# Raw q and k of each head in a tile of its own, two buffers, loaded one head ahead

## The chip, the cores and the metric

The kernel runs on one core of a Trainium2 chip. The metric is the device time of one execution in microseconds (us); the median of three runs is given with its extremes. The core has five engines that run their own instruction streams and wait for each other by semaphores: TensorE (PE; its weight loads are listed as PEld), VectorE (DVE), ScalarE (ACT), GpSimd (POOL) and SyncE (SP). In this kernel SP does nothing but issue DMA transfers, in the order of its stream. A transposition (DMA_TRANSPOSE) is such a transfer too.

## What is computed

Attention with a decay, causal, over 4 batches of 8 heads, 576 positions, head width 64; its output is the input of four experts that are all computed and mixed with given weights.

```python
scores = (q @ k.T) / 8 + (cum[:, None] - cum[None, :])   # cum = cumsum(log(clip(f, 1e-4, 1)))
scores = where(causal, -1e9, scores)
attn   = exp(scores - max(scores)); attn /= sum(attn) + 1e-9
x      = (attn @ v)  -> [2304, 512]                      # 4 x 576 rows, 8 heads x 64
p      = domain_probs / (sum + 1e-9)
out    = sum over e of p[:, e] * (relu(x @ w1[e]) @ w2[e])   # 4 experts, 512 -> 1024 -> 512
```

## The kernel before, in words

**Jobs.** Attention is cut into 32 jobs (`JOBS`, line 42): first, batch by batch, the rows 0 to 255 (half 0), then, batch by batch, the rows 256 to 575 (half 1); within each, four pairs of heads (`pr` 0 to 3, heads `hh` 0 and 1). A name as `pt_2_1_1` is pair 2, half 1, head 1; the digit of the batch is left out where names are printed. In this text, **pair 1 to pair 16** are the jobs of half 1 in the order in which they run: pairs 1 to 4 are batch 0, pairs 5 to 8 batch 1, and so on.

**One head.** Its q and k lie in `raw` (float32, in transposed form, with k below q's positions along the row). ScalarE rounds them to `hi` (line 558), GpSimd makes a copy of q (559) and the remainder of k, `kl` (567; two rows of `kl` with the running decay come by DMA from `ncd`, line 533). PE makes the scores s from `hi` and from `kl` (611), VectorE masks them and takes the row maximum (`p`, `nm`, 625), ScalarE takes exp (640), and ScalarE and VectorE split the result into two float16 halves `z` (706, 707). Three transpositions per head, for the row tiles 2, 3 and 4, turn `z` into `pt` (716, on SP's queue; `z` is 128x6x128, 128x8x128 and 128x9x64). When both heads of a pair are there, PE multiplies `pt` with `v`: 28 matmuls o (809), of which one runs early and 26 or 27 stand together as the **main group o** of the pair, behind the pair's last transposition, which is the 9x64 one of head 1. The result is scaled into `xf` (856).

**The experts.** Four pairs fill a chunk of x. VectorE takes its maximum (`xmax`, 260), a scale is made over PE and back (`topx`, 199 and 220; `ux`, 202 to 232; `xsc`, 249), and ScalarE and VectorE write the chunk as two float16 halves `y` (474, 475). From `y` and the weights PE makes the first layer of the experts (matmuls l, lines 1002 and 1035), with ScalarE and VectorE behind it (`gh`, `gl`, 1015, 1016; `acc`, 1062). Weights come by DMA and are prepared meanwhile (`wr`, `pk`, `wd`, `w`; `wmax` 284; a scale of the weights by `dw` and `tops`, 316 and 317: `dw` goes out to memory, `tops` reads it back). The second half of the execution is the experts alone.

**Loads of `raw`.** The first four jobs' q and k lie in buffers that are free at the start (`first_raw`). From the fifth on `Job.load` (line 505) loads both heads of a job at once into a tile of 128x2x896 float32 of which there is one buffer: 12 loads of 512 KB (half 0), 16 of 896 KB (half 1), each followed by the load of the job's v (`vr`). Since there is one buffer, the transfer of the next job waits until both heads of the job before have been read by ScalarE (558) and GpSimd (559, 567).

**What sets the order.** `head_steps(n)` (line 876) lists the steps that are written while head n is at work: preparation of head n+1, the decay rows of head n+2 (`far`), the load of head n+2's job if that is its first head, then scores, transpositions and o. The steps of the experts are put between them. The order on every engine is then made by the framework's scheduler, which simulates the program's times and takes, on each engine, what it expects to be ready (`schedule_with_timeline_sim=True`, line 1752): other durations or buffers in one place can change the order everywhere, and each engine runs strictly in the order it was given.

Of the kernel before, what the change touches and what calls it, by code (L numbers as in the profile page):

```python
# [8 lines left out]
F32 = mybir.dt.float32  # L9
# [69 lines left out]
def fused(ctx: ExitStack, tc: tile.TileContext, qk, v, f, probs, w, out):  # L79
# [57 lines left out]
    def decays():  # L137
        nc.sync.dma_start(out=fr, in_=f)
        first_loads()
        for t in q2:  # L140
            nc.gpsimd.memset(t[64:66, :].bitcast(F32), 8.0)
        make_identity(nc, ident)
        nc.gpsimd.memset(ones_r, 1.0)
        nc.vector.memset(ones, 1.0)
        nc.vector.tensor_scalar(
            out=fr, in0=fr, scalar1=1e-4, scalar2=1.0, op0=ALU.max, op1=ALU.min
        )
        nc.scalar.activation(out=fr, in_=fr, func=AF.Ln)
        nc.scalar.activation(out=warm, in_=ones[:, :1], func=AF.Exp)
        nc.vector.tensor_tensor_scan(  # L150
            out=ncum, data0=ones, data1=fr, initial=0.0, op0=ALU.mult, op1=ALU.subtract
        )
        nc.scalar.activation(out=nc2[0], in_=ncum, func=AF.Copy)
        nc.vector.tensor_tensor(
            out=nc2[1], in0=ncum, in1=nc2[0].bitcast(F32), op=ALU.subtract
        )
        nc.gpsimd.memset(mask, 0.0)
        nc.gpsimd.affine_select(
            out=mask[:, S - 128 :],
            in_=mask[:, S - 128 :],  # L160
            pattern=[[-1, 128]],
            compare_op=ALU.is_ge,
            fill=NEG,
            base=0,
            channel_multiplier=1,
        )
        for h in range(NEAR):
            jobs[0].near(h)
        for n in range(2):
            nc.sync.dma_start(out=ncd[:, n], in_=nc2[n].bitcast(F32))  # L170
        first_raw(2)
        for j in (0, 2):
            n = 1 if j == 0 else 0
            nc.sync.dma_start(
                out=first_kl[j // 2][64:66, 512 * n :].bitcast(F32).rearrange(
                    "p (h s) -> p h s", s=CH
                ),
                in_=ncd[2 * (j + n) : 2 * (j + 2), :, :CH].rearrange("h n s -> n h s"),
            )
        first_raw(3)  # L180
        w_load(0)
        w_load(1)
        nc.sync.dma_start(out=pr_r, in_=probs)
        jobs[NPR].load()
        for hh in range(2):
            jobs[NPR].far(hh)

    later = {}
# [239 lines left out]
    def first_loads():  # L428

        slots = [  # L430
            x_.tile([128, 1024], F32, tag=t, name=f"first{n}")
            for n, (x_, t) in enumerate([(xf_p, f"xf{k}") for k in range(3)] + [(acc_p, "acc")] * 2)
        ]
        for n in range(2):
            first_kl.append(acc_p.tile([128, 1024], F32R, tag="acc", name=f"kl{n}"))
        vt = slots[3].rearrange("p (r t h d) -> p r t h d", r=NPR, t=2, h=2)
        for j in jobs[:NPR]:
            r = slots[(4, 0, 1, 2)[j.pr]]
            j.raw = r.rearrange("p (h n) -> p h n", h=2)
            j.vr = vt[:, j.pr]  # L440
        first_raw(0)
        nc.sync.dma_start(
            out=slots[3].rearrange("p (r n) -> p r n", r=NPR),
            in_=v[0, :, :, :2].rearrange("r p t h d -> p r (t h d)"),
        )
        first_raw(1)

    def first_raw(n):
        j = jobs[n]
        nc.sync.dma_start(out=j.raw, in_=qk[0, j.pr, :, :, : 2 * CH])  # L450

    xh, xl, xf = {}, {}, {}
    yh, yl = {}, {}
# [38 lines left out]
    class Job:  # L492


        def __init__(self, b, pr, half):
# [4 lines left out]
            self.njt = 2 if half == 0 else 5  # L500
            self.nm = f"{b}_{pr}_{half}"
            self.hi, self.kl, self.q2, self.p, self.nmax = {}, {}, {}, {}, {}
            self.sp, self.last, self.pt, self.tp, self.op = {}, {}, {}, {}, {}

        def load(self):
            b, pr = self.b, self.pr
            n = self.wq + self.wk
            o = 0 if self.half == 0 else CH
            self.raw = raw_p.tile([128, 2, 896], F32, tag="raw", name=f"raw{self.nm}")
            nc.sync.dma_start(out=self.raw[:, :, :n], in_=qk[b, pr, :, :, o : o + n])  # L510
            self.vr = v_p.tile([128, 5, 2, D], F32, tag="vr", name=f"vr{self.nm}", bufs=1)
            nc.sync.dma_start(out=self.vr[:, : self.njt], in_=v[b, pr, :, : self.njt])

        def rows(self, hh):

# [36 lines left out]

        def prep_hi(self, hh):
            wq, wk = self.wq, self.wk
            r = self.raw[:, hh, :]
            hi = hi_p.tile([128, 896], F32R, tag="hi", name=f"hi{self.nm}_{hh}")
            self.hi[hh] = hi
            nc.scalar.activation(out=hi[:, : wq + wk], in_=r[:, : wq + wk], func=AF.Copy)  # L558
# [2 lines left out]
        def prep_lo(self, hh):  # L561
            if hh not in self.kl:
                self.rows(hh)
            wq, wk, ko, qo = self.wq, self.wk, self.ko, self.qo
            r, hi, kl = self.raw[:, hh, :], self.hi[hh], self.kl[hh]
            eng = nc.vector if self is jobs[0] else nc.gpsimd
            eng.tensor_tensor(  # L567
                out=kl[:64, :wk],
# [307 lines left out]
    def head_steps(n):  # L876
# [9 lines left out]
        if n + 2 < len(heads):  # L886
            j, hh = heads[n + 2]
            st.append((0, lambda j=j, hh=hh: j.far(hh)))
        ahead = n + 2 < len(heads) and heads[n + 2][1] == 0
        if ahead:  # L890
            st.append((0, heads[n + 2][0].load))
        qs, ts, us = [], [], []
        if n < len(heads):
            j, hh = heads[n]
# [861 lines left out]
```

## Time and profile before

| | us |
| --- | --- |
| median of 3 runs | 963.48 (958.53 to 964.21) |
| profiled execution | 963.1 |
| its span in the trace | 961.3 |

| engine | busy us | share of the span | instructions |
| --- | --- | --- | --- |
| PE | 895.0 | 93% | 5831 |
| VectorE | 713.9 | 74% | 1458 |
| ScalarE | 559.3 | 58% | 1121 |
| GpSimd | 537.6 | 56% | 544 |

The profiled execution took 1.8 us more than its span, the time from the first recorded instruction to the last. The mean granted clock of PE over the span is 0.988 of full speed. A busy share is an average over stages: attention and the experts' first layer run together up to about 630 us, and the experts alone after that. "Releaser" in a row is what an engine's wait ended with; a row of a timeline with "x27" is so many instructions in succession. In a row of SP's queue the duration is the issue, not the transfer.

### The profile page before, as it was taken

How to read it: one execution, taken by the hardware profiler on the slowest of the kernel's cores; microseconds unless marked ns; L12 is line 12 of the kernel's file. 1: busy time of each engine (PE TensorE's matmuls, PEld its weight loads, DVE VectorE, ACT ScalarE, POOL GpSimd, SP SyncE). 2: the span in 40 equal slices, each digit the busy share in tenths (PEclk: the TensorE clock that was granted, in tenths of full speed). 3: DMA queues.
4: the chain of work that ended last, by engine and by line, in shares of the span. 5: the costliest groups of instructions: out<-in, count | busy, mean ns of one | idle time of the engine just before them, and what ended most of it. 6: DMA issues, size and time to landing. Idle time of an engine off the chain costs nothing.

```text
span 961.3 us, 16609 instructions
## 1 busy us (share of the span) xinstructions
PE 895.0 (93%) x5831; PEld 631.1 (66%) x5831; DVE 713.9 (74%) x1458; ACT 559.3 (58%) x1121; POOL 537.6 (56%) x544
## 2 busy tenths in 40 slices
PE   4799998999998889889899999999998999999998
PEld 3699897999765557556566666654455664566547
DVE  5777675876987988668887877575678847787487
ACT  5777755465767657557566676255656436653350
POOL 4656864567634646325654576163877826686060
PEclk9999999999999999989999999999999999999999
DMA  7458734538989689965998599424313422322003
GB/s 246 140 191 296 254 113 163 187 117 277 279 210 188 175 253 241 226 157 136 259 306 205 116 266 284 117 83 154 110 44 117 147 88 87 111 80 98 23 1 88
DMA packets 147060, 159.45 MB, mean 166 GB/s; under 512 B 85700, under 2 KB 106880, under 8 KB 146976
## 3 DMA queue, kind: packets, MB, share of 16 engines
q1 hardware_dynamic: 146976, 158.39, 57.0%
q8 instruction: 46, 0.75, 0.3%
q14 instruction: 38, 0.31, 0.1%
HBM read 117.30 MB, written 21.65 MB: 145 GB/s over the span
## 4 chain that ended last, share of the span: by engine, by line
PE 19%; POOL 12%; DVE 7%; ACT 5%; issue 4%; DMA 4%; POOLq 0%; DVEq 0%; SPq 0%
PE y L1273 6%; PE m L1273 6%; POOL s L1333 4%; POOL wt L1167 4%; PE l L1002 3%; PE l L1035 3%; POOL wu L1167 2%; DMA pk<-in_w 1%; POOL bs L1199 1%; DVE rl L1154 1%; DMA wr<-in_w 1%; ACT wt L1194 1%; ACT r L1319 1%; DVE acc L1062 1%; DMA raw<-in_qk 1%
## 5 line engine op out<-in xcount | busy, mean ns | idle before, releaser
L1002 PE MATMUL l<-y,w 128*128 128x256 f16 x1248 | 155.9, 275 | 0.0
L640 ACT ACTIVATE p<-p,nm 128x576 f32<-128x576 f32 (+3 forms) x160 | 95.7, 599 | 92.1 <-DVE nm L625 91.3
L1002 PEld LDWEIGHTS <-w 128*128 128x128 f16 x1248 | 118.1, 98 | 30.8 <-issue 6.4
L1035 PE MATMUL l<-w,gh 128*128 128x512 f16 x408 | 123.9, 383 | 5.5 <-ACT w L969 2.8
L707 DVE SCALAR_TENSOR_TENSOR z<-p,z 128x384 f16<-128x384 f32 (+3 forms) x128 | 86.5, 694 | 25.9 <-ACT z L706 24.2
L559 POOL CAST q<-raw 64x320 fp32r<-64x320 f32 (+1 forms) x56 | 27.8, 497 | 127.6 <-PE s L611 63.0
L611 PE MATMUL s<-hi 128*128 128x384 f32 (+1 forms) x192 | 76.7, 403 | 17.0 <-DVE hi L573 8.9
L1062 DVE SCALAR_TENSOR_TENSOR acc<-y,scg,acc 128x256 f32<-128x256 f32 (+1 forms) x164 | 81.1, 515 | 14.9 <-PE y L1273 14.7
L1273 PE MATMUL m<-rh,bs 128*128 128x512 f16 x256 | 86.5, 379 | 3.0 <-ACT r L1319 3.0
L1199 POOL TENSOR_TENSOR bs<-wt,bs 128x512 f16<-128x512 f32 x32 | 38.1, 1194 | 80.4 <-ACT bs L1198 80.2
L625 DVE CUSTOM_DVE_ANT_0 p<-s,mask 128x288 f32<-128x288 f32 (+2 forms) x160 | 74.3, 473 | 10.0 <-PE s L611 9.4
L567 POOL TENSOR_TENSOR kl<-raw,hi 64x576 fp32r<-64x576 f32 (+1 forms) x56 | 66.6, 1189 | 25.5 <-ACT hi L558 24.8
L1035 PE MATMUL l<-w,gl 128*128 128x512 f16 x204 | 77.5, 382 | 0.0
L946 POOL TENSOR_TENSOR wl<-wr,wh 128x512 fp32r<-128x512 f32 x48 | 64.4, 1367 | 16.2 <-ACT wh L942 9.9
L1016 DVE SCALAR_TENSOR_TENSOR gl<-l,gh 128x512 f16<-128x512 f32 (+1 forms) x80 | 54.7, 683 | 25.0 <-ACT gh L1015 24.9
L961 POOL TENSOR_SCALAR wr<-wr,wsc 128x512 f32<-128x512 f32 x32 | 52.5, 1645 | 34.0 <-DMA wr<-in_w 27.8
L1002 PE MATMUL l<-xl,wh 128*128 128x256 f32 x224 | 66.7, 298 | 0.1
L1002 PE MATMUL l<-xh,wh 128*128 128x256 f32 x224 | 66.0, 297 | 0.4
L1273 PE MATMUL m<-rh,bw 128*128 128x512 f16 x191 | 65.2, 383 | 0.8 <-ACT r L1319 0.8
L1002 PE MATMUL l<-xh,wl 128*128 128x256 f32 x224 | 65.7, 293 | 0.0
L1273 PEld LDWEIGHTS <-bs 128*128 128x128 f16 x384 | 37.6, 98 | 41.6 <-issue 3.2
L1035 PEld LDWEIGHTS <-gh 128*128 128x128 f16 x408 | 37.4, 99 | 41.5 <-issue 12.3
(387 smaller groups left out, 2415.6 us busy)
## 6 DMA issues: line engine op xcount, KB each, us to landing
wr<-in_w SPq DMA_DIRECT2D x90, 512.0 KB
pk<-in_w SPq DMA_DIRECT2D x64, 256.0 KB
wd<-w SPq DMA_DIRECT2D x32, 512.0 KB
raw<-in_qk SPq DMA_DIRECT2D x16, 896.0 KB
bw<-wd SPq DMA_DIRECT2D x32, 256.0 KB
bv<-wd SPq DMA_DIRECT2D x32, 256.0 KB
raw<-in_qk SPq DMA_DIRECT2D x12, 512.0 KB
vp<-in_v SPq DMA_DIRECT2D x10, 512.0 KB
```

What stands on the lines that cost most here:

```text
L567: eng.tensor_tensor(out=kl[:64, :wk], in0=r[:64, ko : ko + wk], in1=hi[:64, ko : ko + wk].bitcast(F32), op=ALU.subtract,)
L611: nc.tensor.matmul(out=ps[:, at : at + z - a], lhsT=lhsT, rhs=rhs, start=(m == 0), stop=(m == 1),)
L625: nc.vector.tensor_tensor_reduce(out=pt[:, a:z], in0=ps, in1=mask[:, m0 + a : m0 + z], scale=-0.125, scalar=BIG if n == 0 else nm[:, col : ...
L640: nc.scalar.activation(out=pt[:, :w_], in_=pt[:, :w_], func=AF.Exp, scale=-1.0, bias=self.nmax[hh][:, c : c + 1], accum_out=self.ssum[:, h ...
L707: nc.vector.scalar_tensor_tensor(out=o[:, 1], in0=x, scalar=2.0**14, in1=o[:, 0], op0=ALU.mult, op1=ALU.subtract)
L946: eng.tensor_tensor(out=wl[n][:, a:z], in0=r[:, a:z], in1=wh[n][:, a:z].bitcast(F32), op=ALU.subtract,)
L1002: nc.tensor.matmul(out=self.l1p[:, fi, :], lhsT=lhsT, rhs=rhs[:, k, :], start=(k == 0 and m == 0), stop=(k == 3 and m == 2),)
L1016: self.last = nc.vector.scalar_tensor_tensor(out=self.gl, in0=self.l1p, scalar=0.0, in1=self.gh.bitcast(F32) if wide else self.gh, op0=ALU ...
L1035: matmul(out=l2[tt], lhsT=lhsT, rhs=rhs, start=(self.ps == 0 and fi == 0 and m == 0), stop=(self.ps == 1 and fi == 1 and m == 2),)
L1062: nc.vector.scalar_tensor_tensor(out=acc[c][:, tt, d0:d1], in0=ps, scalar=sc, in1=acc[c][:, tt, d0:d1], op0=ALU.mult, op1=ALU.add,)
L1167: nc.gpsimd.tensor_tensor(out=t[:, k - 1, :], in0=w_of(a), in1=w_of(z), op=op)
L1273: line.append(nc.tensor.matmul(**args))
```

## The change

`raw` becomes a tile of one head, 128x896, and there are two such buffers, in the same space as the one tile before. `Job.load` takes the head `hh` and loads that head's q and k alone; v is still loaded for both heads, with head 0. `head_steps(n)` calls it for each head n+2, so that each head is loaded while head n is at work; before, both heads of a job were loaded at the time of its first head. The loads of `raw` become 56 of half the size (24 of 256 KB, 32 of 448 KB), against 28. The first four jobs' buffers stay, only seen head by head. Preparation reads `self.raw[hh]`.

```diff
@@ before the loop: first loads
-        jobs[NPR].load()
         for hh in range(2):
+            jobs[NPR].load(hh)
             jobs[NPR].far(hh)
@@ first_loads, first_raw
-            j.raw = r.rearrange("p (h n) -> p h n", h=2)
+            j.whole = r.rearrange("p (h n) -> p h n", h=2)
+            j.raw = {hh: j.whole[:, hh] for hh in range(2)}
...
-        nc.sync.dma_start(out=j.raw, in_=qk[0, j.pr, :, :, : 2 * CH])
+        nc.sync.dma_start(out=j.whole, in_=qk[0, j.pr, :, :, : 2 * CH])
@@ class Job
-        def load(self):
+        def load(self, hh):
             b, pr = self.b, self.pr
             n = self.wq + self.wk
             o = 0 if self.half == 0 else CH
-            self.raw = raw_p.tile([128, 2, 896], F32, tag="raw", name=f"raw{self.nm}")
-            nc.sync.dma_start(out=self.raw[:, :, :n], in_=qk[b, pr, :, :, o : o + n])
-            self.vr = v_p.tile([128, 5, 2, D], F32, tag="vr", name=f"vr{self.nm}", bufs=1)
-            nc.sync.dma_start(out=self.vr[:, : self.njt], in_=v[b, pr, :, : self.njt])
+            r = raw_p.tile([128, 896], F32, tag="raw", name=f"raw{self.nm}_{hh}", bufs=2)
+            nc.sync.dma_start(out=r[:, :n], in_=qk[b, pr, :, hh, o : o + n])
+            self.raw[hh] = r
+            if hh == 0:
+                self.vr = v_p.tile([128, 5, 2, D], F32, tag="vr", name=f"vr{self.nm}", bufs=1)
+                nc.sync.dma_start(out=self.vr[:, : self.njt], in_=v[b, pr, :, : self.njt])
@@ prep_hi, prep_lo
-            r = self.raw[:, hh, :]
+            r = self.raw[hh]
@@ head_steps
-        ahead = n + 2 < len(heads) and heads[n + 2][1] == 0
-        if ahead:
-            st.append((0, heads[n + 2][0].load))
+            st.append((0, lambda j=j, hh=hh: j.load(hh)))
```

Lines behind `load` move by 2 to 4: 716 becomes 720, 809 becomes 813, 1002 becomes 1004, 1035 becomes 1037. Numbers at the end of a name only count tiles and differ between the two programs.

The change moves instructions on every engine. Three places are shown, as the programs have them. The first is SP's queue around the last transposition of pair 7 (`pt_2_1_1`, 9x64). Before:

```order
L281 DMA pk_13_5053<-in_w 128x512
L716 DMA_TRANSPOSE pt_2_1_1_4973<-z_2998 128x8x128
L533 DMA kl_0_1_0_5030<-ncd 2x576
L510 DMA raw_0_1_5032<-in_qk 128x2x896
L716 DMA_TRANSPOSE pt_2_1_1_4973<-z_3000 128x9x64
L716 DMA_TRANSPOSE pt_3_1_0_5102<-z_2997 128x6x128
L281 DMA pk_14_5132<-in_w 128x512
```

And after:

```order
L720 DMA_TRANSPOSE pt_2_1_1_5013<-z_3024 128x6x128
L720 DMA_TRANSPOSE pt_2_1_1_5013<-z_3024 128x8x128
L537 DMA kl_0_1_0_5070<-ncd 2x576
L512 DMA raw_0_1_1_5281<-in_qk 128x896
L720 DMA_TRANSPOSE pt_2_1_1_5013<-z_3026 128x9x64
L720 DMA_TRANSPOSE pt_3_1_0_5142<-z_3023 128x6x128
L537 DMA kl_0_1_1_5279<-ncd 2x576
```

The load ahead of that transposition is one head's; the other head's, `raw_0_1_0`, stands 11 rows earlier. The second place is the same queue around the last transposition of pair 8 (`pt_3_1_1`, 9x64). Before:

```order
L716 DMA_TRANSPOSE pt_3_1_1_5299<-z_2998 128x8x128
L316 DMA dw_5414<-wm_5413 128x2
L510 DMA raw_1_1_5364<-in_qk 128x2x896
L317 DMA tops<-dw_5414 128x256
L281 DMA pk_3_5419<-in_w 128x512
L716 DMA_TRANSPOSE pt_3_1_1_5299<-z_3000 128x9x64
L716 DMA_TRANSPOSE pt_0_1_0_5408<-z_2997 128x6x128
```

And after:

```order
L720 DMA_TRANSPOSE pt_3_1_1_5341<-z_3024 128x8x128
L316 DMA dw_5456<-wm_5455 128x2
L512 DMA raw_1_1_1_5582<-in_qk 128x896
L281 DMA pk_3_5461<-in_w 128x512
L720 DMA_TRANSPOSE pt_3_1_1_5341<-z_3026 128x9x64
L720 DMA_TRANSPOSE pt_0_1_0_5450<-z_3023 128x6x128
L317 DMA tops<-dw_5456 128x256
```

`tops`, which reads what `dw` has written, has moved from ahead of the last transposition to two places behind it, and the load of `raw` between is half as large. The third place is PE's stream between the main groups o of pair 4 and pair 5, from the scores of `s_1_1_0` on. Before:

```order
L611 MATMUL s_1_1_0_2_0_4468<-hi_1_1_0_4330 128x384
L611 MATMUL s_1_1_0_2_0_4468<-kl_1_1_0_4133,q_0_116 128x384
L1035 LDWEIGHTS gh_1_3_0_4513
L1035 MATMUL l_1_1_3_0_0_4629<-w_3626,gh_1_3_0_4513 128x512
L611 MATMUL s_1_1_0_3_0_4498<-hi_1_1_0_4330 128x512
L611 MATMUL s_1_1_0_3_0_4498<-kl_1_1_0_4133,q_0_116 128x512
L1035 LDWEIGHTS gl_1_3_0_4514
L1035 MATMUL l_1_1_3_0_0_4629<-w_3626,gl_1_3_0_4514 128x512
L220 MATMUL topx_178<-ux_179,ones_r 128x1
L1035 LDWEIGHTS gh_1_3_0_4513
L1035 MATMUL l_1_1_3_0_1_4636<-w_3618,gh_1_3_0_4513 128x512
```

And after:

```order
L615 MATMUL s_1_1_0_2_0_4504<-hi_1_1_0_4364 128x384
L615 MATMUL s_1_1_0_2_0_4504<-kl_1_1_0_4167,q_0_116 128x384
L615 MATMUL s_1_1_0_3_0_4534<-hi_1_1_0_4364 128x512
L615 MATMUL s_1_1_0_3_0_4534<-kl_1_1_0_4167,q_0_116 128x512
L220 MATMUL topx_178<-ux_179,ones_r 128x1
L615 MATMUL s_1_1_0_4_0_4563<-hi_1_1_0_4364 128x288
L615 MATMUL s_1_1_0_4_0_4563<-kl_1_1_0_4167,q_0_116 128x288
L615 MATMUL s_1_1_0_4_1_4566<-hi_1_1_0_4364 128x288
L615 MATMUL s_1_1_0_4_1_4566<-kl_1_1_0_4167,q_0_116 128x288
L813 LDWEIGHTS v_0_1_4159
L813 MATMUL o_0_1_4612<-pt_0_1_0_4220,v_0_1_4159 64x320
```

The matmuls of the experts (1035) that stood between the scores now stand further ahead, before the main group of pair 4; between that group and the first matmul on the next `y` there are 156 matmuls before, 100 of them of the experts, and 26 after, none of the experts.

## Rows read from the trace of the kernel before

**Rows 1.** The page's first part: busy us, share of the span, instructions of each engine.
```profile
PE 895.0 (93%) x5831; PEld 631.1 (66%) x5831; DVE 713.9 (74%) x1458; ACT 559.3 (58%) x1121; POOL 537.6 (56%) x544
```
**Rows 2.** Busy time by stretches: stretch, length, PE, PEld, DVE, ACT, POOL, granted clock, DMA share, GB/s.
```profile
48.00:240.00 192.00, 186.63 (x1231) 170.74 (x1231) 137.54 (x329) 121.79 (x271) 125.41 (x139) 0.99 0.59 199
240.00:432.00 192.00, 168.71 (x1198) 119.83 (x1197) 157.62 (x356) 122.52 (x252) 93.22 (x89) 0.97 0.86 217
```
**Rows 3.** Tile `raw`: its loads (ns of issue: least/median/most), and all waits for it (us, times).
```profile
L510 SPq DMA_DIRECT2D raw<-in_qk x28: 549/565/900, 14.7 to 567.1; - x28
...
  DMA raw<-in_qk: 64.6, 28
```
**Rows 4.** PE's waits: what waited, on what, us in all, times, longest.
```profile
PE o L809 <- DMA pt<-z: 18.5, 7, 4.1
...
PE s L611 <- POOL hi L573: 2.3, 2, 1.2
```
**Rows 5.** Timeline around pair 7, SP's queue and PE: start, us, engine, line, operation.
```profile
394.06 0.58 SPq L510 DMA_DIRECT2D raw<-in_qk  x1
394.74 2.61 SPq L716 DMA_TRANSPOSE pt<-z  x2
...
402.30 1.98 PE L809 MATMUL o<-pt,v 128*64 128x320 f16 x18 [3.63 <-DMA pt<-z]
```
**Rows 6.** Timeline around pair 8, SP's queue and PE.
```profile
419.37 0.53 SPq L316 DMA_DIRECT2D dw<-wm  x1
419.99 0.57 SPq L510 DMA_DIRECT2D raw<-in_qk  x1
...
423.06 0.33 SPq L317 DMA_DIRECT2D tops<-dw  x1
...
423.92 1.28 SPq L716 DMA_TRANSPOSE pt<-z  x1
...
429.21 2.08 PE L809 MATMUL o<-pt,v 128*64 128x320 f16 x14 [4.14 <-DMA pt<-z]
```
**Rows 7.** Timeline around pair 5, SP's queue and PE.
```profile
353.94 1.21 SPq L716 DMA_TRANSPOSE pt<-z  x1
...
356.92 1.69 PE L809 MATMUL o<-pt,v 128*64 128x320 f16 x27 [3.20 <-DMA pt<-z]
...
359.75 1.49 PE L1002 MATMUL l<-y,w 128*128 128x256 f16 x12
```
**Rows 8.** Timeline of PE: the main groups o of pairs 2 and 4.
```profile
292.23 1.69 PE L809 MATMUL o<-pt,v 128*64 128x320 f16 x27 [2.65 <-DMA pt<-z]
...
330.36 2.31 PE L809 MATMUL o<-pt,v 128*64 128x320 f16 x27 [3.84 <-DMA pt<-z]
```
**Rows 9.** Timeline of VectorE (DVE) from pair 4's o to `y`.
```profile
333.57 0.88 DVE L546 SCALAR_TENSOR_TENSOR v<-vr,vsc,v 128x640 f16<-128x640 f32 x1 [0.19 <-ACT v L545]
...
337.57 0.55 DVE L856 TENSOR_TENSOR xf<-o,rw 128x256 f32<-128x256 f32 x2
338.04 1.21 DVE L260 TENSOR_REDUCE xmax<-xf 128x1 f32<-128x1024 f32 x1
340.42 0.69 DVE L1016 SCALAR_TENSOR_TENSOR gl<-l,gh 128x512 f16<-128x512 f32 x1 [1.17 <-ACT gh L1015]
...
356.12 1.39 DVE L1062 SCALAR_TENSOR_TENSOR acc<-l,scg,acc 128x512 f32<-128x512 f32 x2
357.48 1.28 DVE L475 SCALAR_TENSOR_TENSOR y<-xf,xsc,y 128x1024 f16<-128x1024 f32 x1
```
**Rows 10.** The page's groups: line, operation, times, busy us, mean ns, idle before it.
```profile
L707 DVE SCALAR_TENSOR_TENSOR z<-p,z 128x384 f16<-128x384 f32 (+3 forms) x128 | 86.5, 694 | 25.9 <-ACT z L706 24.2
...
L625 DVE CUSTOM_DVE_ANT_0 p<-s,mask 128x288 f32<-128x288 f32 (+2 forms) x160 | 74.3, 473 | 10.0 <-PE s L611 9.4
```
**Rows 11.** The chain of waits, 548 to 556 us: start, us, what ran, times.
```profile
550.15 1.96 PE l L1035 x9
...
553.24 1.98 PE l L1002 x18
```

More of the change, by code (lines that the diff above doesn't have):

```diff
@@ L502, in __init__ @@
             self.hi, self.kl, self.q2, self.p, self.nmax = {}, {}, {}, {}, {}
+            self.raw = {}
             self.sp, self.last, self.pt, self.tp, self.op = {}, {}, {}, {}, {}
-        def load(self):
+        def load(self, hh):
             b, pr = self.b, self.pr
@@ L564, in prep_lo @@
             wq, wk, ko, qo = self.wq, self.wk, self.ko, self.qo
-            r, hi, kl = self.raw[:, hh, :], self.hi[hh], self.kl[hh]
+            r, hi, kl = self.raw[hh], self.hi[hh], self.kl[hh]
             eng = nc.vector if self is jobs[0] else nc.gpsimd
```

## Prediction

> **What bounds the kernel now.** The page's first part comes first: TensorE (PE) is busy 895.0 of 961.3 us, no other engine above 74% [rows 1]. So the time moves in two ways only: PE is given less idle time, or more. The busy time by stretches says where the idle time is: 192 − 186.63 = 5.4 us from 48 to 240 us, 192 − 168.71 = 23.3 us from 240 to 432 [rows 2]. The second of these stretches is the one to read.
>
> The change is about the load of `raw`, so the waits for it come next. All engines together wait 64.6 us in 28 places for `raw` [rows 3], which looks like the prize. But none of that is PE's. What PE needs from a `raw` is made by ScalarE and GpSimd (`hi`, `kl`), and PE's own waits show 2.3 us in 2 places for `hi` [rows 4]; both lie before 48 us, where the first four pairs are still fed from other buffers. What PE does wait for is the transposition that turns `z` into `pt`: 18.5 us in 7 places in front of the matmuls o [rows 4]. The direct gain of an earlier `raw` is therefore taken as nothing: an engine that waits for `raw` here has time to wait.
>
> What is left is indirect: a `raw` transfer stands on SP's queue among the transpositions, and the scheduler, given other loads, puts everything into another order. Both are terms of the sum.
>
> **Term 1: the transfer in front of a transposition.** Undisturbed, a last transposition is issued at 353.94 and PE has its data at 356.92: 2.98 us [rows 7]. In pair 7 the load of `raw` (two heads, 896 KB) is issued at 394.06, the transposition at 394.74, and o starts at 402.30, 7.56 us later; 3.63 us of it is PE's idle time [rows 5]. The excess is 7.56 − 2.98 = 4.6 us. I read it as the time in which the transposition's packets stand behind those of `raw`. A load of one head is half of it, so half of 4.6, 2.3 us, should come back. In the order after, the load that stands there is one head's.
>
> In pair 8 the order is `dw`, `raw`, `tops`, transposition, at 419.37, 419.99, 423.06 and 423.92, and o starts at 429.21 [rows 6]. Two things are late. SP issues in order, and `tops` has to wait for `dw` to land, so the transposition behind it waits from 420.56 (the end of `raw`'s issue, 419.99 + 0.57) to 423.92. And from there it takes 5.29 us, 2.3 more than 2.98; half of that excess is 1.15. After the change `tops` stands behind the transposition, so of the 423.92 − 420.56 = 3.4 us all but an issue of about half a microsecond goes: 2.9. 1.15 + 2.9 = 4.0, of the 4.14 us that PE waits. Term 1 is −2.3 − 4.0 = **−6.3 us**. It cannot give more than the two waits, 3.63 + 4.14 = 7.8, and gives nothing if the transfer wasn't the cause.
>
> The 28 added transfers cost SP an issue each. One takes 565 ns [rows 3]; 28 × 0.57 = 16 us of SP's time, on a queue that issues ahead and has gaps. That is nothing on PE, except where an issue stands right in front of a last transposition, about half a microsecond each time, inside the bounds.
>
> **Term 2: the order on PE.** While attention's matmuls wait, PE is fed with matmuls of the experts (l, lines 1002 and 1035), and they run out at the end of a batch, until the next `y` is made. I counted them in the order of PE's instructions before and after, between the main groups o of the pairs. They cost 0.11 us (L1002) and 0.217 us (L1035) each: 1.98 / 18 and 1.96 / 9 [rows 11].
> - Up to pair 1: 12 and 12 more (12 × 0.11 + 12 × 0.217 = 3.9), 4 matmuls s fewer (−0.8): +3.1.
> - Pair 1 to pair 3: 19 more of L1002, 2.1 us. The first 13 stand where PE is idle 2.65 us ahead of pair 2 [rows 8]: 0, and 2.1 if not absorbed.
> - Pair 3 to pair 4: 21 and 36 more, 2.3 + 7.8 = 10.1, and 4 matmuls s more, 0.8: 10.9. They fill the 3.84 us that PE waits ahead of pair 4 [rows 8]: +7.1.
> - What has been done early is missing later. From pair 4's o to the first matmul on the new `y`, PE has 156 matmuls before, 100 of them of the experts; after, 26 small ones and none of the experts. This stretch is 359.75 − 330.36 = 29.4 us now [rows 7, 8], and PE is full in it but for 3.2 us. After the change it lasts as long as the chain on VectorE that makes `y`: xf, xmax, the scale, y, with the passes p and z of two heads in between.
>
> How long that chain is, no row shows. Below: the passes that stand in it by the order, 8 × 0.473 (p) + 5 × 0.694 (z) [rows 10] + 0.88 (v) + 1.21 (xmax) + 1.28 (y) [rows 9] = 10.6 us, with no wait at all. Above: as now, 359.75 − (330.36 + 2.31) = 27.1. Between them: from xf's start to the first l it is 359.75 − 337.57 = 22.2 now, and 8 passes for the experts that stand in it (340.42 to 356.12, together 5.6 us) [rows 9] go; v, 0.88, comes in: 17.5. I take this, since it keeps the waits between the engines as the trace shows them; nothing then delays xf itself. With o's 2.31 the stretch is 19.8 instead of 29.4: −9.6 (bounds −16.5 and 0).
> - Pair 5's o, which now lies inside that stretch, comes after it: 1.69 us of work [rows 7], and its last z ends about 1.97 us ahead of y's end (one more z, 0.69 [rows 10], and y's 1.28). Its transposition needs 2.98, and in the order a `raw` stands ahead of it, 2.3: PE idles 2.98 + 2.3 − 1.97 = 3.3. Together +5.0 (1.7 if the transposition is in time).
>
> Term 2 is 3.1 + 0 + 7.1 − 9.6 + 5.0 = **+5.6 us**; the bounds are 3.1 + 7.1 − 16.5 + 1.7 = −4.6 and 3.1 + 2.1 + 7.1 + 0 + 5.0 = +17.3. From pair 6 to the end, PE's order is nearly the same, and there is no more term.
>
> **Sum.** The profiled execution took 963.1 us, 0.4 below the median of 963.48. 963.1 − 6.3 + 5.6 = **962.4 us**. The two terms are of like size and opposite sign, which is why I expect no change that can be measured (about 1% is what a measurement of this kernel can tell from none).
>
> **The rivals.**
> A. The forecast, both terms near their middle: 962.4, own range 954 to 969. Chance 0.42.
> B. The change doesn't do for the transpositions what it should: they are late for another reason than the size of a `raw` load. For it: pair 2 and pair 4 wait 2.65 and 3.84 us as well [rows 8]. Against it: 2.98 against 7.56 us, with the load between [rows 5, 7]. Term 1 is then 0 and pair 5's wait has no 2.3: 963.1 + 3.3 = 966.4. Chance 0.14.
> C. Slower: PE runs dry at pair 5 as the order says, and the chain to `y` isn't shorter than now, because it hangs on waits between the engines (exp, z, the scale's way over PE and back) and not on the passes that go. Then what was done early is never given back: 963.1 − 6.3 + 17.3 = 974.1. It decides (over 973.1) from a chain of 26.1 us on. For it: VectorE is busy only 82% (157.62 of 192) in this stretch although it has work [rows 2]. Against it: 5.6 us of passes do go. Chance 0.17.
> D. Faster: the passes run through with few waits, and all transpositions of these pairs are in time: 963.1 − 7.8 − 4.6 = 950.7. For it: every matmul that goes early goes into a place in which PE waits today, and the work itself doesn't grow. Against it: a chain of 10.6 us without a wait is found nowhere in the rows. Chance 0.24.
> E. Every added transfer puts its own way on the path. From `dw`'s issue to `tops`, which waits for it, is 423.06 − 419.37 = 3.7 us [rows 6]; 28 × 3.7 = 103, so 1066. Against it: the next transfer is issued 0.68 us behind a `raw` [rows 5], they overlap, and no pass of PE waits for a `raw`. Chance 0.03.
>
> The Trainium skill has a rule on the side of E: its page "DMA: Bandwidth & Descriptors" gives about 2.0 us of fixed cost for a DMA of any size (section "Anatomy of one DMA — SWDGE (gpsimd) path", another issue path than the one used here) and says to batch DMAs to 1 MiB or more (section "Bandwidth"). By this page the split would cost an estimated 28 × 2.0 = 56 us, 1019 us in all, if none of it were hidden. The trace doesn't bear it out as a cost of the whole: the issue spacing of 0.68 us says that it is hidden [rows 5].
>
> **How the numbers follow.** 962.4 is A's sum, and A is the likeliest. The range reaches to D below and C above: 948 to 975. It leaves out E (0.03), the part of D below 948 and the part of C above 975 (some 0.07 each). Faster by over 1% (under 953.8) is most of D and a tail of A: 0.25. Slower by over 1% (over 973.1) is most of C, E and a tail of A: 0.17. Within 1%: 0.58.
>
> **What would show it.** Right: 56 loads of `raw`, of about 0.57 us issue each; the time from the last transposition's issue to o about 5 us in pair 7 and in pair 8; `tops` behind the transposition in pair 8; a hole on PE between pair 4 and the first l of the next chunk, with the stretch near 20 us, and more l ahead of pair 4. Wrong: pair 7 still at 7.5 us (term 1 falls, B); the stretch near 29 us (C) or near 13 (D); PE waiting for `hi` after 48 us, which would mean that the halved loads come too late, a wait that the sum doesn't have at all. A time outside the range would most likely come from the order after pair 6, which I take as unchanged: each of the eleven pairs left has a transposition that needs only to slip by a few microseconds to move the sum.

## The result and the profile after

The change makes the kernel slower: 969.45 us (median of 6 runs, 966.9 to 969.89) against 961.4 us before (6 runs), a ratio of 1.0078 with a 95% interval of 1.0058 to 1.0098. The forecast was 962.4. What the change says it does, it does: 56 loads go out, and the list of waits around `raw` has no row for its transfer any more, where it was 64.6 us [rows 3]. The prize that the view of waits shows was won in full, and the time went up, by little, but clear of the noise.

The profile after, page part 1, then the busy time by stretches (columns as in [rows 2]), the loads of `raw`, and PE's waits:

```profile
PE 898.9 (93%) x5831; PEld 630.9 (65%) x5831; DVE 712.9 (74%) x1458; ACT 556.4 (57%) x1121; POOL 536.2 (55%) x544
```
```profile
48.00:240.00 192.00, 187.44 (x1258) 172.55 (x1259) 135.49 (x334) 121.28 (x272) 128.89 (x140) 0.98 0.64 208
240.00:432.00 192.00, 168.01 (x1152) 116.37 (x1152) 155.36 (x347) 118.80 (x247) 88.51 (x86) 0.93 0.85 206
432.00:624.00 192.00, 184.05 (x1340) 125.23 (x1337) 150.09 (x324) 119.51 (x245) 100.58 (x92) 0.97 0.82 210
```
```profile
L512 SPq DMA_DIRECT2D raw<-in_qk x56: 327/366/1265, 14.3 to 570.3; - x56
```
```profile
PE o L813 <- DMA pt<-z: 11.8, 6, 3.2
PE s L615 <- DVE hi L577: 8.8, 1, 8.8
PE l L1037 <- DVE acc L1064: 8.4, 9, 2.5
...
PE topx L199 <- DVE xmax L260: 5.6, 1, 5.6
```

PE's waits for `pt` fell from 18.5 to 11.8 us [rows 4]. In their place stand waits for VectorE (`acc`, 8.4 us, where it was 2.7) and one wait of 5.6 us for `xmax`. PE is busy 3.9 us longer with the same instructions, and its granted clock between 240 and 432 us is 0.93 instead of 0.97.

Since the order on PE differs, equal times are not equal progress. So I went through both traces by work: every matmul counts with the usual spacing to the next one of its kind and shape (the 20th percentile over both traces), and time minus work done is what PE has lost so far. After minus before, at equal work:

| place (time before) | what lies behind it | lost, after minus before | change |
| --- | --- | --- | --- |
| 142 us | half 0 | −4.2 | −4.2 |
| 274 us | ahead of pair 1 | −4.0 | +0.2 |
| 342 us | behind pair 4 | −11.4 | −7.4 |
| 371 us | behind pair 5 | +5.9 | +17.3 |
| 437 us | behind pair 8 | +2.2 | −3.7 |
| 544 us | behind pair 12 | +3.2 | +1.0 |
| 599 us | behind pair 15 | +7.1 | +3.9 |
| end | | +6.7 | −0.4 |

The table holds one trace of each, and executions scatter: e10 below, whose order is that of the change up to 328 us, stands at −1.6 and 0.0 in the first two rows. So rows of up to 4 us show a loss only where other runs repeat it. The two large ones are repeated: the four other runs with the new order around pair 4 and the loads of the change have −8.0 to −9.2 and +15.3 to +17.9 (e4, e6, e11, e13). So is the row of pair 15: +2.2 to +4.2 from 544 to 599 us in the other runs that keep the new order there (e3, e6, e10, e11).

The −7.4 and +17.3 belong together: matmuls l that run ahead of pair 4 fill waits there, and are missing behind it. PE there, after (timeline, around the main group of pair 4, which starts at 340.42), VectorE's stream in the same place, and the busy time of two stretches:

```profile
340.42 1.72 PE L813 MATMUL o<-pt,v 128*64 128x320 f16 x27
347.77 0.37 PE L199 MATMUL topx<-ident,xmax 128*1 128x128 f32 x1 [5.64 <-DVE xmax L260]
...
358.32 0.59 PE L1004 MATMUL l<-y,w 128*128 128x256 f16 x2
361.61 3.20 PE L813 MATMUL o<-pt,v 128*64 128x320 f16 x27 [2.71 <-DMA pt<-z]
364.74 3.48 PE L1004 MATMUL l<-y,w 128*128 128x256 f16 x20
```
```profile
342.17 0.55 DVE L860 TENSOR_TENSOR xf<-o,rw 128x256 f32<-128x256 f32 x2 [0.90 <-PE o L813]
345.91 0.69 DVE L284 TENSOR_REDUCE wmax<-pk 128x1 f32<-128x512 f32 x1 [3.18 <-DMA pk<-in_w]
346.51 1.21 DVE L260 TENSOR_REDUCE xmax<-xf 128x1 f32<-128x1024 f32 x1
...
359.67 1.27 DVE L476 SCALAR_TENSOR_TENSOR y<-xf,xsc,y 128x1024 f16<-128x1024 f32 x1
```
```profile
342.00:348.00 6.00, 0.36 (x6) 0.25 (x4) 2.65 (x5) 0.83 (x1) 1.56 (x1) 0.88 0.59 203
348.00:364.00 16.00, 11.90 (x48) 8.39 (x49) 15.42 (x41) 13.39 (x30) 6.77 (x9) 0.50 0.58 132
```

This is the hole that the order showed. Two things are seen beside its idle time: VectorE's `xmax` stands behind a `wmax` that waits 3.18 us for a load of weights, and after the idle 5.64 us PE's granted clock is 0.50 (the lower level, 1.2 GHz), so that pair 5's main group takes 3.20 us where it took 1.69 [rows 7]. What either costs is not parted from the hole by these rows; `xmax` ahead of `wmax` was not tried.

### The profile page after: what moved, and what is told of

It reads as the page before. It is cut to its first block, busy times and chain, and to the rows that moved or that the text cites. A ratio compares the mean times of both kernels' runs of the same rounds, so it can differ in the third digit from the quotient of the medians.

```text
span 967.9 us, 16697 instructions
## 1 busy us (share of the span) xinstructions
PE 898.9 (93%) x5831; PEld 630.9 (65%) x5831; DVE 712.9 (74%) x1458; ACT 556.4 (57%) x1121; POOL 536.2 (55%) x544
## 4 chain that ended last, share of the span: by engine, by line
PE 51%; DVE 13%; DMA 12%; POOL 10%; ACT 6%; issue 5%; SPq 1%; DVEq 0%; POOLq 0%; ACTq 0%
PE l L1004 14%; PE l L1037 13%; PE y L1275 8%; PE m L1275 7%; DMA pk<-in_w 5%; POOL s L1335 4%; PE s L615 3%; POOL wt L1169 3%; DMA pt<-z 3%; PE o L813 2%; DMA wr<-in_w 2%; DVE z L711 2%; DVE acc L1064 2%; POOL wu L1169 1%; DVE p L629 1%
## 5 line engine op out<-in xcount | busy, mean ns | idle before, releaser
L711 DVE SCALAR_TENSOR_TENSOR z<-p,z 64x64 f16<-64x64 f32 (+3 forms) x128 | 90.7, 728 | 22.9 <-ACT z L710 21.3
L963 POOL TENSOR_SCALAR wr<-wr,wsc 128x512 f32<-128x512 f32 x32 | 55.3, 1732 | 42.8 <-DMA wr<-in_w 37.4
L615 PE MATMUL s<-kl,q 66*128 66x384 f32 (+1 forms) x192 | 64.1, 338 | 1.6 <-DMA kl<-nc 1.6
```

The source lines that it names most:

```text
L615: nc.tensor.matmul(out=ps[:, at : at + z - a], lhsT=lhsT, rhs=rhs, start=(m == 0), stop=(m == 1),)
L711: nc.vector.scalar_tensor_tensor(out=o[:, 1], in0=x, scalar=2.0**14, in1=o[:, 0], op0=ALU.mult, op1=ALU.subtract)
L963: nc.gpsimd.tensor_scalar(out=r[:, c], in0=r[:, c], scalar1=sc, scalar2=None, op0=ALU.mult)
```

## Experiments

Two questions are mixed in the change: other loads, and another order of everything, since the scheduler plans anew. To separate them the order was held. From a built program I took, engine by engine, the order of all instructions but the loads of `raw`, and gave it to the other program as edges that fix the issue order and add no wait:

```diff
+    for e, to in ORDER.items():        # PE, VectorE, ScalarE, GpSimd, SP; places in the source
+        for a, b in zip(to, to[1:]):
+            tc.add_manual_dep(stream[e][b], stream[e][a].name, no_sync)
```

Below, "old" is the order of before and "new" the order after; a mixed order takes the one up to a place and the other for all that is left. All ratios are to the kernel before, from runs on the same chip, with their 95% intervals.

**Loads or order.** e1: `-ORDER made by the scheduler`, `+ORDER = old`, on the changed kernel.

> The loads of the change (one head each, two buffers), but every other instruction of each engine in the order that it has before; only the loads of raw stand where the scheduler puts them. Theory ORDER (the time is lost by the order that the scheduler makes, the loads themselves give a little back): 961.4 less half a burst in front of the last transposition of pair 7 (2.3) and of pair 8 (1.15), so 958, and no hole on PE behind pair 4. Rival LOADS (twice as many, smaller transfers cost the time, by their issues, their fixed cost or where they land): about 969, as the changed kernel.

e2: the same with the kernel before and `+ORDER = new`.

> The loads of before (both heads at once, one buffer), but every other instruction of each engine in the order that it has after the change. Theory ORDER: 969.5 or, with whole bursts in pairs 7 and 8 again (2.3 and 1.15), 973; the hole behind pair 4 is there. Rival LOADS: about 961, as before.

e1: 960.77, ratio 0.9974 (0.9957 to 0.9992). e2: 1019.0, ratio 1.0568 (1.0534 to 1.0602). So the new loads with the old order cost nothing and give a little: LOADS falls, and the whole loss of the change, 1.0078 against 0.9974, lies in the order. e2 missed its number by far. The new order is no order for the old loads: ScalarE, which now has the preparation of a head earlier in its stream, stands still until the load of both heads is there, and everything behind it with it (ScalarE's wait for `raw` in e2, which was 16.3 us before):

```profile
ACT hi L560 <- DMA raw<-in_qk: 84.8, 20, 9.6
```

An order is made for the arrival times that the scheduler expects; it isn't good or bad by itself.

**Which part of the order.** e3 and e4 cut at pair 6, e5 and e6 just ahead of pair 3, with the loads of the change: `+ORDER = old to pair 6, then new` (e3), `new to pair 6, then old` (e4), `new to pair 3, then old` (e5), `old to pair 3, then new` (e6).

> The loads of the change; the order of before up to the first matmul o of pair 6, the order after the change from there on. Theory ORDER, with the loss where the trace after has it: no hole behind pair 4, so the 5.4 us that PE has lost up to pair 6 go, and what the later order costs (about 4 us at pair 15) stays: 963. If all of the loss sits ahead of pair 6: 960. Rival LOADS: 969.

> The loads of the change; the order after the change up to the first matmul o of pair 6, the order of before from there on. Theory ORDER, with the loss where the trace after has it: the hole behind pair 4 stays (5.4 us), the loss at pair 15 (about 4 us) goes: 965. If all of the loss sits ahead of pair 6: 969. Rival LOADS: 969.

> The loads of the change; the order after the change up to just before the main group of pair 3 (some 42 matmuls l run early), the order of before from there on: 85 matmuls l between pair 3 and pair 4, 100 between pair 4 and pair 5. Theory RUN-OUT (the loss is that the matmuls l are used up between pairs 3 and 4 and PE has none behind pair 4): no hole, 961 as the run with the order of before. Rival EARLY (what costs is the order ahead of pair 3): 967.

> The loads of the change; the order of before up to just before the main group of pair 3, the order after the change from there on: 142 matmuls l between pair 3 and pair 4, 2 between pair 4 and pair 5. Theory RUN-OUT: the hole behind pair 4 is back, 967 to 969. Rival EARLY: 961.

| run | us | ratio | interval |
| --- | --- | --- | --- |
| e1 old | 960.77 | 0.9974 | 0.9957 to 0.9992 |
| e3 old to pair 6, new | 960.58 | 0.9975 | 0.9954 to 0.9995 |
| e4 new to pair 6, old | 966.90 | 1.0051 | 1.0030 to 1.0071 |
| e5 new to pair 3, old | 963.97 | 1.0012 | 0.9987 to 1.0038 |
| e6 old to pair 3, new | 966.01 | 1.0052 | 1.0024 to 1.0079 |

Ahead of pair 6 the new order costs 0.77% (e4 less e1); behind pair 6 alone it costs nothing (e3). Ahead of pair 3 it costs 0.38% (e5), from pair 3 on 0.78% (e6): neither RUN-OUT nor EARLY is the only cause, though with intervals of some ±0.3% on such differences the 0.38% is barely clear of nothing. Ahead of pair 3, one new wait is seen in the trace after, at pair 1 (SP's queue, VectorE, and PE), where before PE did not wait:

```profile
273.48 0.35 SPq L316 DMA_DIRECT2D dw<-wm  x1
276.80 0.32 SPq L317 DMA_DIRECT2D tops<-dw  x1
277.21 3.12 SPq L720 DMA_TRANSPOSE pt<-z  x2
```
```profile
274.02 2.60 DVE L711 SCALAR_TENSOR_TENSOR z<-p,z 64x512 f16<-64x512 f32 x2
```
```profile
282.17 2.08 PE L813 MATMUL o<-pt,v 128*64 128x320 f16 x14 [3.17 <-DMA pt<-z]
```

It looks like pair 8's trouble of before [rows 6], `tops` waiting for `dw` in front of a transposition, but it isn't: VectorE ends the `z` that is turned only at 274.02 + 2.60 = 276.62, so the queue holds the transposition up for 0.6 us. Nor does this wait account for the 0.38%. Counted as in the table, e5 and e1 stand level behind pair 1 (−3.0 each at 300 us), and e5 falls 3.1 us behind by 312 us, at pair 3, where its order changes over. What costs in e5 stays open; it may be the change-over itself.

**The run-out by itself.** e10 is the changed kernel with the scheduler free, and one rule: the last 57 of the matmuls l that went ahead of pair 4 have to issue behind its main group.

```diff
+    for n in HELD:                     # 57 matmuls l
+        tc.add_manual_dep(pe[n], pe[LAST_O].name, no_sync)
```

> The changed kernel with one rule for the scheduler and all else free: the last 57 of the matmuls l that moved ahead of pair 4's main group have to stay behind it. Between pairs 3 and 4 there are then 85 matmuls l as before, between 4 and 5 there are 59 instead of 2, and the order elsewhere is that after the change. Theory RUN-OUT: the hole behind pair 4 closes, 969.45 - 4.8 = 964.7, ratio to before 1.003. Rival EARLY (all of the loss comes from the order ahead of pair 3): no gain, 1.008.

964.49, ratio 1.0021 (1.0001 to 1.0040), as expected: 0.57% come back when this hole is closed. The order that the scheduler made is that of the change everywhere but between 328 and 428 us. In the trace the wait for `xmax` is gone; PE waits ahead of pair 4 again, even longer than before (7.98 us, where it was 3.84 [rows 8]), and its main group runs at the lower clock (3.19 us), and still it is cheaper, since pair 5 then waits 0.43 us instead of 2.71:

```profile
340.33 3.19 PE L813 MATMUL o<-pt,v 128*64 128x320 f16 x27 [7.98 <-DMA pt<-z]
...
360.67 0.60 PE L813 MATMUL o<-pt,v 128*64 128x320 f16 x6 [0.43 <-DMA pt<-z]
```

**The clock in the hole.** e11 fills the hole of the changed kernel with work for nothing, order held to the new one:

```diff
+            for _ in range(48):        # ahead of topx of this chunk
+                nc.tensor.transpose(ps[:, 384:512], mask[:, :128], ident)
```

> The order and loads after the change, with 48 transpositions of a constant tile on PE (0.108 us each, 5.2 us in all, into a part of PSUM that nobody reads) in the hole between pair 4's main group and the matmul topx: PE does work that serves nothing, nothing else changes. Theory CLOCK (part of the loss is that the granted clock falls to 0.5 after the hole, and the 16 matmuls s, the o group and the 20 matmuls l behind it run at that clock): the granted clock stays near 1.0 from 346 to 367 and 2 to 4 us come back, 966. Rival CHAIN (VectorE's chain to y sets the length, PE's clock doesn't matter): 969.5.

968.05, ratio 1.0061 (1.0039 to 1.0083), where the change has 1.0078 (1.0058 to 1.0098). The stretches 340 to 346, 346 to 362 and 362 to 368 us of e11, and then the same three after:

```profile
340.00:346.00 6.00, 6.00 (x65) 5.83 (x59) 1.81 (x4) 0.83 (x1) 1.56 (x1) 1.00 0.59 211
346.00:362.00 16.00, 8.17 (x37) 5.38 (x37) 15.85 (x42) 13.01 (x30) 6.79 (x9) 0.70 0.65 121
362.00:368.00 6.00, 6.00 (x51) 4.77 (x46) 2.48 (x5) 1.33 (x3) 0.00 (x0) 0.66 0.93 203
```
```profile
340.00:346.00 6.00, 2.13 (x30) 1.43 (x27) 1.81 (x5) 0.83 (x1) 1.56 (x1) 1.00 0.85 271
346.00:362.00 16.00, 10.13 (x33) 7.25 (x35) 15.48 (x39) 11.45 (x26) 6.77 (x9) 0.52 0.50 113
362.00:368.00 6.00, 6.00 (x47) 4.53 (x44) 4.12 (x10) 2.91 (x7) 0.00 (x0) 0.58 1.07 181
```

The clock stayed up for some microseconds more (0.70 instead of 0.52) and fell in the next waits all the same. PE's matmuls s got shorter and PE only waited longer: VectorE is busy 15.85 of 16 us there. This speaks for CHAIN as far as the matmuls s go. The rest of CLOCK was not put to the test: pair 5's main group still ran at the lower level (3.19 us in e11's trace, 3.20 after), so what that costs stays open. The gain of 0.17% is inside the intervals.

**Term 1 by itself.** e7 is e1 with the last transpositions of pairs 7 and 8 ahead of what stood in front of them on SP's queue:

```diff
 pair 7:  kl
-         raw_0_1_1
          DMA_TRANSPOSE pt_2_1_1 128x9x64
+         raw_0_1_1
 pair 8:  dw
-         raw_1_1_1, tops, pk
          DMA_TRANSPOSE pt_3_1_1 128x9x64
+         raw_1_1_1, tops, pk
```

> The loads of the change, the order of before on every engine, and on SP's queue two moves: in pair 7 the load of raw stands behind the last transposition instead of ahead of it; in pair 8 the load of raw, tops and one pk stand behind it. Theory BURST (what is issued ahead of the last transposition makes it late): PE's waits of 1.4 us (pair 7) and 5.0 us (pair 8) go, 960.8 - 6.4 = 954.4, the time from issue to o about 3 us where PE waits for it at all. Rival OTHER (the transposition is late for another reason than what stands ahead of it): 961 and waits of about the same length.

960.28, ratio 0.9983 (0.9953 to 1.0012): no gain over e1 (0.9974). Yet the moves did what they should. PE's waits ahead of pairs 7 and 8 were 1.43 and 4.97 us in e1 (its rows first); in e7 they are gone, pair 8 starts 5.1 us earlier, and what comes instead is seen in PE's next wait, in VectorE's wait behind it, and in PE's waits for the whole of e7:

```profile
399.69 1.72 PE L815 MATMUL o<-pt,v 128*64 128x320 f16 x27 [1.43 <-DMA pt<-z]
...
425.85 2.58 PE L815 MATMUL o<-pt,v 128*64 128x320 f16 x18 [4.97 <-DMA pt<-z]
```
```profile
397.86 1.72 PE L814 MATMUL o<-pt,v 128*64 128x320 f16 x27
...
420.75 1.72 PE L814 MATMUL o<-pt,v 128*64 128x320 f16 x27
...
426.59 0.59 PE L1038 MATMUL l<-w,gh 128*128 128x512 f16 x2 [2.02 <-DVE acc L1065]
```
```profile
424.76 0.69 DVE L285 TENSOR_REDUCE wmax<-pk 128x1 f32<-128x512 f32 x1 [2.32 <-DMA pk<-in_w]
```
```profile
PE l L1038 <- DVE acc L1065: 15.6, 9, 4.2
...
PE o L814 <- DMA pt<-z: 5.6, 2, 3.4
```

BURST is right on the spot and wrong in the sum: 15.6 us of waits for `acc` where e1 had 8.6. VectorE's stream now sets the pace, with its own waits in it. One of them is of e7's own making: `wmax`, which stands ahead of `acc`, waits 2.32 us for the `pk` that e7 had moved behind the transposition. e14 below leaves `pk` where it was and gains nothing either, so this isn't all. By pair 10, e7's lead over e1 is down from 5.1 to 1.6 us. PE's time at one wait is worth only what the next engine behind lets through.

**Late in the attention.** e8 takes the new order only where it gained (from pair 6 to pair 14), e12 adds the two moves of `raw`, e13 is the new order up to pair 14 and the old behind it (`+ORDER = old to 6, new to 14, old`; `the same, raw behind the transposition in pairs 7 and 8`; `new to 14, old`).

> The loads of the change; the order of before up to the first o of pair 6, the order after the change from there to pair 14, the order of before from there on. If the order after the change costs only in two places, behind pair 4 and at pair 15, this leaves both out: 960.6 less the 4.3 us that the trace of the run with the old order to pair 6 loses at pair 15: 956. If the loss at pair 15 is only what was gained before, given back: 960.6.

> As the run with the order of before up to pair 6 and from pair 14 on and the order after the change between (957.4), and on SP's queue the loads of raw of pairs 7 and 8 go behind the last transposition. Theory BURST: PE's waits for those transpositions (2.3 and 3.0 us) shrink by 1.8 us each, 954. Theory GIVEN BACK (the next wait, for VectorE's acc, takes what is won, as in the run with the transposition first): 957.

> The loads of the change; the order after the change up to pair 14, the order of before from there on. Theory PAIR 15 (the changed order costs about 4 us a second time at pair 15, where VectorE waits 2.5 us for a w that stands ahead of gl): 969.45 - 4 = 965.5, ratio 1.004. Rival GIVEN BACK (what is lost at pair 15 is lost in any case): 1.008.

e8: 957.42, ratio 0.9946 (0.9919 to 0.9973). e12: 958.52, 0.9942 (0.9912 to 0.9971), again nothing from the moves, although on the spot they do what BURST says: at pair 7, where PE waits for the transposition in both, it takes 5.39 us from its issue to o in e8, with the load ahead of it, and 3.08 us in e12, with the load behind it. e13: 963.32, 1.0013 (0.9988 to 1.0038): against the change, 0.65% come back when the order from pair 14 on is the old one. PE's own order is the same in e13 as in the change; the other engines' differs, in a dozen places from 573 us on. At pair 15 the new VectorE stream has `w` ahead of `gl`, and `w` waits for ScalarE (the trace after first, VectorE and PE; then before, where `gl` went first):

```profile
586.31 0.75 DVE L972 SCALAR_TENSOR_TENSOR w<-wr,wsc,w 128x512 f16<-128x512 f32 x1 [2.51 <-ACT w L971]
586.98 0.68 DVE L1018 SCALAR_TENSOR_TENSOR gl<-l,gh 128x512 f16<-128x512 f32 x1
```
```profile
596.24 1.01 PE L1037 MATMUL l<-w,gh 128*128 128x512 f16 x2 [2.54 <-DVE acc L1064]
```
```profile
580.51 0.69 DVE L1016 SCALAR_TENSOR_TENSOR gl<-l,gh 128x512 f16<-128x512 f32 x1 [1.36 <-ACT gh L1015]
...
582.21 0.75 DVE L970 SCALAR_TENSOR_TENSOR w<-wr,wsc,w 128x512 f16<-128x512 f32 x1
```

Whether the parts add up can't be said: 0.57% (e10) and 0.65% (e13) make 1.22%, against 1.04% between e1 and the change, each with an interval of some ±0.3%. e3, whose tail is the new one, is no slower than e1. Counted as in the table, its trace loses 4.5 us from 570 to 599 us, at pair 15, as well, but it has gained 5.6 us between 371 and 400 us, where the new order begins.

**The split alone.** e9 leaves every place as before and makes two transfers of one, each into a tile of its own as in the change:

```diff
-  raw_0_1     <- in_qk 128x2x896
+  raw_0_1_0   <- in_qk 128x896
+  raw_0_1_1   <- in_qk 128x896
```

> Two loads of one head each, standing one behind the other where the load of both heads stood before; every other instruction of each engine in the order of before. So the number and the size of the transfers change, not the place. Theory ARRIVAL (what the loads give with the old order, 0.26%, comes from head 0's load going earlier): as before, ratio 1.000. Rival SPLIT (smaller transfers with a semaphore of their own do it): 0.997. Rival ISSUE (28 more issues cost): above 1.003.

e14 adds the moves of e7 (without pk). e15 is the kernel before with two transfers into its one tile and the scheduler free:

```diff
-            nc.sync.dma_start(out=self.raw[:, :, :n], in_=qk[b, pr, :, :, o : o + n])
+            for hh in range(2):
+                nc.sync.dma_start(out=self.raw[:, hh, :n], in_=qk[b, pr, :, hh, o : o + n])
```

> As the run with two loads in the place of one (956.6), and on SP's queue the loads of raw in pair 7, and the loads of raw and tops in pair 8, go behind the last transposition; pk stays ahead of it. Theory BURST: PE's waits of 2.1 us (pair 7) and 5.8 us (pair 8) go and stay gone, 949. Theory GIVEN BACK (the next engine's wait takes it within two pairs): the waits for pt go, waits for VectorE's acc come, 956.

> The kernel before with one edit: the load of raw is issued as two transfers, one for each head, into the one tile of before, at the same step of the program; the scheduler orders everything anew. Between pairs 3 and 4 there are then 105 matmuls l, between 4 and 5 there are 46. Theory SPLIT AND RUN-OUT (the split gives 0.75% and the hole takes what the missing matmuls l leave open, here about half of the 4.8 us): 956.6 + 2.4 = 959, ratio 0.995. Rival ISSUE (more transfers cost): above 1.003. Rival ORDER ONLY (any new order loses as much as the changed one did): 1.008.

e9: 956.61, ratio 0.9925 (0.9900 to 0.9950), the lowest of the study, though e8, e12 and e14 lie within the intervals. e14: 954.69, 0.9928 (0.9908 to 0.9948), once more no gain from the moves. All three theories of e9 missed: SPLIT had the sign, and less than half the size. e15: 965.45, ratio 1.0045 (1.0021 to 1.0070), slower than before. It is two transfers as well, but not the same split: they fill one tile, and the engines wait for `raw` as before (64.6 us in 28 places [rows 3]), where e9's two tiles leave 41.6 us in 15 (e15 first, then e9):

```profile
  DMA raw<-in_qk: 65.2, 28
```
```profile
  DMA raw<-in_qk: 41.6, 15
```

So the 1.2% between e9 and e15 hold two differences, the order and the tiles, and no run parts them: two transfers into one tile under the old order were not tried. What stands is e9 against before.

Why the split gives more without the early loads (e9) than with them (e1) isn't settled. One difference is seen: a load that stands early on SP's queue waits there until its buffer is free, and what stands behind it waits too. SP's waits ahead of loads of `raw`, in e1 and in e9; before, there are three such rows with 9.6, 7.4 and 2.0 us:

```profile
SPq L513 <- POOL hi L579: 23.8, 18, 2.7
```
```profile
SPq L513 <- POOL hi L578: 12.8, 13, 2.0
```

That this is the cause was not tried.

## Why the prediction was wrong, step by step

The forecast was a small gain, from two terms of like size; the time went up by 0.78%. The mechanisms of the second term are in the trace, but the sum is off by 7 us, in four steps. What is measured below is the difference of the two traces at equal work, from the table.

- **"The direct gain of an earlier `raw` is therefore taken as nothing."** It isn't nothing. With the old order held (e1) PE has lost 4.6 us less than before by 142 us, as after (4.2). The scatter is large, but all fifteen traces with loads of one head (those of the change and of every run but e2) have lost less there than the one trace of before, by 1.2 to 4.8 us. Not all of it lasts: e1 ends at −1.7, and its ratio is 0.9974. PE has no wait for `hi` there, as I said (I left out one of 8.9 us, at the start, which is 8.8 after). It loses the time in pieces of at most 0.7 us ahead of matmuls and weight loads (`s`, t, o, l, `topx`). That they come from ScalarE's waits for `raw` (1.3 and 1.2 us, from 85 to 100 and from 100 to 125 us, none in e1), which push back what stands behind them in its stream, is argued and not shown. A stretch before, and the same after:

```profile
95.00:100.00 5.00, 4.50 (x34) 4.15 (x33) 2.85 (x7) 3.67 (x6) 4.28 (x5) 1.00 0.91 337
```
```profile
95.00:100.00 5.00, 5.00 (x34) 4.51 (x34) 4.29 (x11) 3.79 (x9) 4.55 (x5) 1.00 0.98 274
```

- **Term 1, −6.3.** Measured after: −3.7 between pair 5 and pair 8. Half the burst brought pair 7 from 7.56 to 406.71 − 400.95 = 5.76 us, near the 5.3 expected; pair 8 took 431.19 − 424.62 = 6.57, where 4.1 was expected, with a load of weights in front of it on the queue and the next transposition behind. After, SP's queue and PE at pair 7, then at pair 8:

```profile
393.61 6.31 SPq L720 DMA_TRANSPOSE pt<-z  x2
...
400.95 2.58 SPq L720 DMA_TRANSPOSE pt<-z  x2
...
406.71 1.95 PE L813 MATMUL o<-pt,v 128*64 128x320 f16 x27 [2.67 <-DMA pt<-z]
```
```profile
424.62 2.55 SPq L720 DMA_TRANSPOSE pt<-z  x2
...
431.19 2.52 PE L813 MATMUL o<-pt,v 128*64 128x320 f16 x27 [2.61 <-DMA pt<-z]
```

At pair 7 I also counted from the wrong point. VectorE had the last `z` ready at 392.06 before and at 397.47 after; the queue took it only at 394.74 and 400.95, because SP was still issuing the transposition ahead of it (for 3.2 us before, 4.2 after), and then `kl` and `raw`. From `z` to o it is 10.24 and 9.24 us, so 1.0 us came back and not 1.8. More important, the term is no term of the sum: e7, e12 and e14 take these waits away or shorten them, and the time stays. I priced a wait by its length and did not ask what VectorE lets PE do next.
- **Term 2, +5.6.** Places and counts were right: 2 matmuls l behind pair 4, a stretch of 358.32 − 340.42 = 17.9 us (19.8 forecast), 2.71 us idle ahead of pair 5 (3.3). The size was not: +9.9 from 274 to 371 us (−4.0 to +5.9). Missing from the sum were the halved clock behind the hole, 1.5 us for pair 5's main group and 1.3 for the 20 matmuls l (0.174 us each instead of 0.11), which no run priced by itself, and the wait at pair 1, which I had not priced because nothing waited there before. e10 puts the hole itself at 0.57%, about 5.5 us.
- **"From pair 6 to the end, PE's order is nearly the same, and there is no more term."** This failed outright. Counted again, between pairs 10 and 11 there are 141 matmuls l instead of 106, between 11 and 12 there are 79 instead of 102, and VectorE's stream at pair 15 differs as shown. It is +4.9 us from pair 8 to pair 15 and +4.5 to the end, and e13 shows that it is the order. At pair 15 I could not have seen it on PE, whose order is the same there; I had compared PE's stream alone.

−4.2 + 0.2 − 7.4 + 17.3 − 3.7 + 1.0 + 3.9 − 0.4 = +6.7, against −0.7 forecast. By steps the forecast was off by −4.0 (the direct gain), +2.6 (term 1), +4.3 (term 2) and +4.5 (behind pair 8). That it was off by no more is luck: the gain that I had put at nothing hides part of the rest.

The profiled execution after took 969.7 us, between rivals B (966.4) and C (974.1). C (PE runs dry at pair 5 and nothing gives it back) had the right place, but its reason, a chain as long as before, did not hold. B had term 1 at nothing, and so it is, but not for B's reason: a smaller burst does bring the transposition forward (e8 and e12), and it is worth nothing. Rival E is refuted: with the order held, 28 more transfers come out at 0.9925 and 0.9974. The Trainium skill's page "DMA: Bandwidth & Descriptors", section "Bandwidth", has the rule quoted ahead, to batch DMAs to 1 MiB or more. The runs with the order held don't bear it out as a cost here: 896 KB in two pieces, each with a tile of its own, was faster than in one (e9). That a piece can be used when it lands would explain it, and fewer waits for `raw` (41.6 us against 64.6) fit; but in e1 these waits are all but gone (1.5 us) and the gain is smaller, so the reason stays open.

## What to carry to other kernels

Where a scheduler orders the program, a change of a load is two changes; hold the order (issue-only edges from the old program) to see what the load itself does, before you judge it, and compare the streams of all engines, not only of the busiest. A wait is worth its length only if the engine behind it has slack: take it away once by hand and look for where the time comes back. Work that runs ahead to fill one wait is missing at the next place that has nothing else, here at the end of a batch; count what is left there.

## What was not expected of the hardware

A DMA transposition of the same 128x9x64, counted from its issue to the first matmul that waited for it, took 2.98 us at pair 5 before [rows 7] and 3.08 us at pair 7 in e12, with no load of 256 KB or more issued in the last microsecond ahead of it and one of 448 to 896 KB issued 1.3 us behind. It took 5.0 to 7.6 us at pairs 7 and 8 (before, after and e1), with a load of 256 to 896 KB issued within 0.7 us ahead. The issue of a transposition by itself, 1.2 us at most places, held SP's queue for 3.2 us (before) and 4.2 us (after) ahead of pair 7's last one.

After 5.6 us without work PE's granted clock was 0.50 for the next 16 us. Filling those 5.6 us kept it at 1.00 only until the next waits, and the time did not move beyond the intervals (e11).
